# Two of the output sums of a seven-product channel mix move from VectorE to GpSimd

## The chip, the cores and the metric

The kernel runs on one core of one Trainium2 chip. The metric is the device time of one execution in microseconds (us). The kernel before takes 271.89 us, the median of three runs (271.51 to 272.08). The profiled execution of it has a span of 269.8 us, counted from its first to its last instruction; all times in the profile lines below are counted from that start.

A core has several engines that run side by side and wait for each other by semaphores: TensorE (PE in the profile, PEld for its weight loads) multiplies matrices into PSUM banks; VectorE (DVE), ScalarE (ACT) and GpSimd (POOL) do elementwise work; SyncE (SP) mostly issues DMA transfers.

## The reference

Eight batches of 576 tokens, 8 heads of 64. A linear attention with cosine weights gives x, and an MLP mixer follows: a token mix, a residual, a channel mix and a second residual.

```python
q_p = phi(q, cos_w, sin_w)            # relu(q) * cos, relu(q) * sin
k_p = phi(k, cos_w, sin_w)
kv  = np.einsum('bhsf,bhsd->bhfd', k_p, v)
num = np.einsum('bhsf,bhfd->bhsd', q_p, kv)
den = np.einsum('bhsf,bhf->bhs', q_p, k_p.sum(axis=2))[..., None] + 1e-06
x   = num / den                        # then heads side by side: [8, 576, 512]

h  = np.maximum(x.transpose(0, 2, 1) @ w_tok1, 0.0) @ w_tok2
u  = x + h.transpose(0, 2, 1)
h2 = np.maximum(u @ w_ch1, 0.0) @ w_ch2
return u + h2
```

The change concerns the last two lines: h1 = relu(u @ w_ch1) (1536 wide), the product h1 @ w_ch2, and the sum u + h2.

## The kernel before

512 tokens of each batch are worked on as one channel call; the remaining 64 tokens of all eight batches form a last call, the tail (`u_tail`). The first calls (batches 0 and 1) are written out in a list of operations; batches p = 2 to 7 and the tail go through `channel7`, seven calls in all. While the call of batch p runs, `hooks7` puts work of later batches into its slots: attention, token mix and residual of batch p + 1 (so for p = 2 to 6), features of q and k and the casts of v for batch p + 2 (p = 2 to 5), loads of batch p + 3.

`channel7` computes h1 @ w_ch2 in seven half-size products instead of eight (Winograd's form of Strassen's scheme). h1 is cut into four quadrants: a11 and a12 are the two channel halves of the upper 256 tokens, a21 and a22 those of the lower 256. The output tile u is cut into u11, u12, u21, u22 in the same way by tokens and output columns. Each quadrant of u is 128 x 512 in fp32.

```python
        for mi in range(NCH):                       # 12 up-projections, TensorE
            c_ps = psM.tile([P, 512], F32, name="c_ps", tag="psM")   # 4 banks in turn
            ...                                     # c_ps += wc1 x uT
            relu(by_slot[mi], h1[:, mi, :], c_ps)   # ScalarE or VectorE
            ...                                     # s1 = a21 + a22, s2 = s1 - a11 (VectorE, L652)
            step()                                  # the hooks of this slot
        Dk = bank()
        ...
            A = bank()
            product(A, a11, quad(0, 0), True)
            nc.scalar.copy(va, A)                   # L686
        nc.vector.tensor_sub(a21, a11, a21)         # L687
        step()
        product(Dk, a22, t4, True)
        nc.scalar.copy(vb, Dk)                      # L690
        nc.vector.tensor_sub(u22, u22, vb)          # L691
        step()
        Bk = bank()
        product(Bk, s2, t2, True)
        nc.vector.tensor_add(va, Bk, va)            # L695
        nc.vector.tensor_sub(s2, a12, s2)           # L696
        step()
        C = bank()
        product(C, s1, t1, True)
        nc.scalar.copy(vc, C)                       # L700
        nc.vector.tensor_add(u12, u12, va)          # L701
        nc.vector.tensor_add(u22, u22, vc)          # L702
        step()
        product(Dk, a21, t3, False)
        nc.vector.tensor_add(vb, Dk, va)            # L705
        step()
        wide = ...                                  # vb, read once for each column half
        u2 = ...                                    # u21 and u22 together
        product(C, s2, quad(1, 1), False)           # the sixth product: needs L696
        if fine:                                    # the tail
            nc.vector.tensor_add(u2, u2, wide)      # L711
            store(2, u, 2)
            nc.vector.tensor_add(u12, C, u12)       # L713
            store(0, u, 2, slice(D2, Dm))
            ...
            for jj in range(2):
                product(A, a12, quad(1, 0), False, (jj,))
                nc.vector.tensor_add(u11[:, jj], A[jj], u11[:, jj])   # L718
            ...
        else:
            nc.vector.tensor_add(u12, C, u12)       # L721
            step()
            product(A, a12, quad(1, 0), False)
            nc.vector.tensor_add(u11, A, u11)       # L724
            store(0, u, 2)
            nc.vector.tensor_add(u2, u2, wide)      # L726
            store(2, u, 2)
```

All matmuls of these products are at L657 in the profile, those of the up-projection at L667. The profile calls `va` w2r (it lives in the memory of that weight), a quadrant of h1 `h`, and s1 and s2 both `s`.

Other parts that matter here: the residual of the next batch and its bf16 cast for the transposing DMA, put in slots 10 and 11 of the call, just ahead of the seven products:

```python
        def uo(self, g):                            # VectorE, L466
            nc.vector.tensor_add(self.sb("u")[:, js, :], self.ps.pop(("u", g)), self.x[:, js, :])
        def ubc(self, g, eng="P"):                  # GpSimd, ub<-u
            copy(eng, self.sb("ub")[:, js, :], self.u[:, js, :])
        def utx(self, g):                           # SyncE, L473: uT<-ub, for the next call
            nc.sync.dma_start_transpose(...)
        def turnx(self, j, n):                      # SyncE, L355: qpT<-qp
            nc.sync.dma_start_transpose(...)
        def feat(self, t, j, g, f, eng): ...        # q and k features, ScalarE L331, VectorE L333
        def cast(self, a, n, g, eng): ...           # v to bf16, vbf<-vt, mostly GpSimd
```

The qp tile has one buffer: features of the next batch can be written only once the transposes have read it.

Of the kernel before, what the change touches and what calls it, by code (L numbers as in the profile page):

```python
# [59 lines left out]
def kernel(  # L60
# [11 lines left out]
    nc = tc.nc  # L72
# [555 lines left out]
    def channel7(uT, u, store, by_slot, hooks, fine=False):  # L628
# [3 lines left out]
        def step():  # L632
            nonlocal slot
            for f in hooks.get(slot, ()):
                f()
            slot += 1
# [8 lines left out]
        vb = one.tile([P, 2, D2], F32, name="vb")  # L645
        vc = one.tile([P, 2, D2], F32, name="vc")
        u11, u12 = u[:, 0:2, :D2], u[:, 0:2, D2:]
        u21, u22 = u[:, 2:4, :D2], u[:, 2:4, D2:]
# [39 lines left out]
        step()  # L688
        product(Dk, a22, t4, True)
        nc.scalar.copy(vb, Dk)  # L690
        nc.vector.tensor_sub(u22, u22, vb)  # L691
        step()
        Bk = bank()
        product(Bk, s2, t2, True)
# [4 lines left out]
        product(C, s1, t1, True)  # L699
        nc.scalar.copy(vc, C)  # L700
        nc.vector.tensor_add(u12, u12, va)  # L701
        nc.vector.tensor_add(u22, u22, vc)  # L702
        step()
        product(Dk, a21, t3, False)
        nc.vector.tensor_add(vb, Dk, va)  # L705
# [124 lines left out]
    for p in range(2, B):  # L830
        s = bt[p]
        n = bt[p + 1] if p + 1 < B else None
        m = bt[p + 2] if p + 2 < B else None
        nxt = p + 3 if p + 3 < B else None
        if p < QUADS:
            channel(s.uT, s.u, store_batch(p), evac, hooks_for(n, m, nxt))
        else:
            channel7(s.uT, s.u, store_batch(p), evac7 if n else evac2, hooks7(n, m, nxt, p == QUADS))
    channel7(uT_tail, u_tail, store_tail, evac2, {}, fine=True)

    _ = tile, bass_utils
# [30 lines left out]
```

## Time and profile before

| what | value |
|---|---|
| time, median of 3 runs | 271.89 us |
| span of the profiled execution | 269.8 us |
| granted TensorE clock | 0.993 |
| VectorE busy | 207.4 us, 381 instructions |
| GpSimd busy | 52.8 us, 68 instructions |
| L691, u22 - vb, p = 2 to 7 | 6 instructions, 8.3 us |
| L702, u22 + vc, p = 2 to 7 | 6 instructions, 4.1 us |
| the same two in the tail | 0.69 and 0.69 us |

How to read it: a busy share is an average over the whole span. A group line names the source line, the engine, the operation, out<-in, the shape, the count, the busy total, the mean in nanoseconds and the idle time ahead of it with what ended it. A line of the waits names who waited, for whom, for how long in total, how often, and the longest. A timeline line begins with start and duration in us. DVE instructions overlap by about 0.08 us where one follows another, so starts and ends touch with a small overlap.

### The profile page before, as it was taken

How to read it: one execution, taken by the hardware profiler on the slowest of the kernel's cores; microseconds unless marked ns; L12 is line 12 of the kernel's file. 1: busy time of each engine (PE TensorE's matmuls, PEld its weight loads, DVE VectorE, ACT ScalarE, POOL GpSimd, SP SyncE). 2: the span in 40 equal slices, each digit the busy share in tenths (PEclk: the TensorE clock that was granted, in tenths of full speed). 3: DMA queues.
4: the chain of work that ended last, by engine and by line, in shares of the span. 5: the costliest groups of instructions: out<-in, count | busy, mean ns of one | idle time of the engine just before them, and what ended most of it. 6: DMA issues, size and time to landing. Idle time of an engine off the chain costs nothing.

```text
span 269.8 us, 5452 instructions
## 1 busy us (share of the span) xinstructions
PE 255.2 (95%) x2165; PEld 160.9 (60%) x2181; DVE 207.4 (77%) x381; ACT 143.8 (53%) x236; POOL 52.8 (20%) x68
## 2 busy tenths in 40 slices
PE   6987999999999999999999999999999999999991
PEld 2875556456444556765676557655765575585580
DVE  6389798799791879969896869796968596584592
ACT  2886272384491577739772878287833423323410
POOL 2164060040023261202432013220300030000000
PEclk9999999999999999999999999999999999999997
DMA  6999999999999999799999995950492053003004
GB/s 201 358 234 155 254 255 209 345 252 232 332 294 181 304 374 360 137 166 331 268 334 183 317 362 119 169 186 2 92 222 116 0 80 156 19 2 156 0 2 157
DMA packets 79145, 53.41 MB, mean 198 GB/s; under 512 B 47760, under 2 KB 76688, under 8 KB 79120
## 3 DMA queue, kind: packets, MB, share of 16 engines
q1 hardware_dynamic: 74544, 48.77, 68.2%
q0 software_dynamic: 4144, 3.77, 9.3%
q10 hardware_dynamic: 432, 0.52, 0.5%
q8 instruction: 17, 0.28, 0.4%
q14 instruction: 8, 0.07, 0.1%
HBM read 35.85 MB, written 9.44 MB: 168 GB/s over the span
## 4 chain that ended last, share of the span: by engine, by line
PE 62%; DVE 22%; DMA 8%; issue 4%; ACT 1%; SPq 1%; DVEq 0%; ACTq 0%
PE c_ps L667 21%; PE m_ps L657 10%; PE c L513 8%; PE o L525 7%; DMA kt<-in_k_dram 6%; PE b L434 5%; DVE u L466 4%; DVE s L652 4%; PE kv L362 3%; DVE u L691 3%; PE nf L391 2%; DVE s L696 2%; PE u L461 2%; DVE kp L333 2%; DVE w2r L695 1%
## 5 line engine op out<-in xcount | busy, mean ns | idle before, releaser
L667 PE MATMUL c_ps<-uT,wc 128*128 128x512 bf16 x288 | 70.4, 379 | 0.6 <-ACT h L269 0.3
L269 ACT ACTIVATE h<-c_ps 128x512 bf16<-128x512 f32 x66 | 39.3, 595 | 52.5 <-PE c_ps L667 32.9
L667 PEld LDWEIGHTS <-wc 128*128 128x128 bf16 x336 | 30.9, 98 | 32.8 <-issue 0.6
L657 PEld LDWEIGHTS <-h 128*128 128x128 bf16 x336 | 32.9, 98 | 5.3
L265 POOL CAST ub<-u 128x1024 bf16<-128x1024 f32 x14 | 18.5, 1327 | 84.2 <-DVE u L466 45.6
L331 ACT ACTIVATE qp<-qt,cos_t 128x512 bf16<-128x512 f32 x33 | 23.3, 719 | 21.3 <-DMA qt<-in_q_dram 12.7
L657 PEld LDWEIGHTS <-s 128*128 128x128 bf16 x252 | 24.2, 98 | 6.8 <-DVE s L696 4.0
L271 DVE TENSOR_SCALAR h<-c_ps 128x512 bf16<-128x512 f32 x18 | 12.4, 689 | 20.1 <-PE c_ps L667 20.0
L265 POOL CAST vbf<-vt 128x512 bf16<-128x512 f32 (+3 forms) x28 | 18.1, 680 | 42.8 <-DMA vt<-in_v_dram 42.0
L657 PE MATMUL m_ps<-wc,s 128*128 128x256 bf16 x168 | 20.7, 273 | 2.6 <-DVE s L696 2.6
L513 PE MATMUL c<-uT,wc 128*128 128x512 bf16 x96 | 22.7, 379 | 0.1
L525 PE MATMUL o<-wc,h 128*128 128x512 bf16 x92 | 21.6, 379 | 0.2
L414 DVE TENSOR_TENSOR x<-nf,den 128x512 bf16<-128x512 f32 x30 | 20.7, 691 | 1.0
L331 ACT ACTIVATE qp<-qt,sin_t 128x512 bf16<-128x512 f32 x30 | 21.4, 722 | 0.0
L391 PEld LDWEIGHTS <-qpT 128*128 128x128 bf16 x320 | 15.2, 98 | 10.1 <-DVE x L414 1.5
L657 PE MATMUL m_ps<-wc,h 128*128 128x256 bf16 x168 | 20.6, 273 | 0.0
L657 PE MATMUL m_ps<-t,h 128*128 128x256 bf16 x168 | 20.6, 273 | 0.0
L434 PE MATMUL b<-x,w 128*128 128x512 bf16 (+1 forms) x84 | 19.8, 353 | 0.3
L466 DVE TENSOR_TENSOR u<-u,x 128x1024 f32<-128x1024 f32 x16 | 19.3, 1216 | 0.8 <-PE u L461 0.8
L331 ACT ACTIVATE kp<-kt,sin_t 128x512 bf16<-128x512 f32 x21 | 14.8, 714 | 3.1 <-DMA kt<-in_k_dram 3.1
L461 PE MATMUL u<-B,w 128*128 128x512 bf16 x64 | 16.1, 379 | 0.0
L333 DVE TENSOR_SCALAR kp<-kt,cos_t 128x512 bf16<-128x512 f32 x18 | 10.7, 599 | 6.7 <-DMA kt<-in_k_dram 6.7
(117 smaller groups left out, 375.8 us busy)
## 6 DMA issues: line engine op xcount, KB each, us to landing
out_dram<-u SPq DMA_DIRECT2D x32, 256.0 KB, 3.7
qt<-in_q_dram SPq DMA_DIRECT2D x8, 640.0 KB, 7.4
kt<-in_k_dram SPq DMA_DIRECT2D x8, 640.0 KB, 8.0
qt<-in_q_dram SPq DMA_DIRECT2D x8, 512.0 KB, 6.3
kt<-in_k_dram SPq DMA_DIRECT2D x8, 512.0 KB, 6.9
vt<-in_v_dram SPq DMA_DIRECT2D x6, 640.0 KB, 8.8
vt<-in_v_dram SPq DMA_DIRECT2D x6, 512.0 KB, 7.4
wc<-in_moe_w_ch_dram POOLq DMA_DIRECT2D x4, 384.0 KB, 8.7
```

What stands on the lines that cost most here:

```text
L265: (nc.scalar.copy if eng == "A" else ENG[eng].tensor_copy)(dst, src)
L269: nc.scalar.activation(dst, src, AF.Relu)
L331: nc.scalar.activation(dst, src, AF.Relu, scale=tab)
L391: nc.tensor.matmul(nm[:, hh * (D + 1):(hh + 1) * (D + 1)], self.qpT[:, j * H + h, :], self.kv[:, h, :D + 1], start=(not eps or hh == 0), s ...
L414: nc.vector.tensor_mul(dst, nmv[:, :, :, :D], den_b)
L434: nc.tensor.matmul(b1[:, mi], w1[:, col(self.c, j), mi * P:(mi + 1) * P], self.x[:, j, cs], start=(j == 0 and (g == 2 or mi == 0)), stop=( ...
L461: nc.tensor.matmul(ps[:, jj], w2[:, ki, 1 + 2 * g + jj, :], self.B1[:, ki, :], start=(ki == 0), stop=(ki == NT - 1))
L466: nc.vector.tensor_add(self.sb("u")[:, js, :], self.ps.pop(("u", g)), self.x[:, js, :])
L513: nc.tensor.matmul(ps, wc1[:, ki, mi * P:(mi + 1) * P], self.uT[:, :, ki, :], start=(ki == 0), stop=(ki == NCC - 1))
L525: nc.tensor.matmul(self.ps["o", j], self.h1[:, ki, j * P:(j + 1) * P], wc2[:, ki, :], start=(ki == 0), stop=(ki == NCH - 1))
L657: nc.tensor.matmul(ps[jj] if isinstance(ps, list) else ps[:, jj], a[:, ki, jj * P:(jj + 1) * P], b[:, ki], start=(first and ki == 0 and (j ...
L667: nc.tensor.matmul(c_ps, wc1[:, ki, mi * P:(mi + 1) * P], uT[:, :, ki, :], start=(ki == 0), stop=(ki == NCC - 1))
```

## The change

Two of the output sums, u22 = u22 - vb and u22 = u22 + vc, are computed by GpSimd instead of VectorE, at the same places of the program. All their inputs and their output lie in SBUF, which GpSimd can read: ScalarE has already copied the PSUM banks into vb and vc. Everything else stays, the last sum of that quadrant included (`u2 += wide`, on VectorE, L726 or L711), which now waits for GpSimd. It is for taking work from VectorE, which in this phase also prepares the operands a21 and s2 of the later products, and giving it to an engine that has less to do.

```diff
         step()
         product(Dk, a22, t4, True)
         nc.scalar.copy(vb, Dk)
-        nc.vector.tensor_sub(u22, u22, vb)
+        nc.gpsimd.tensor_sub(u22, u22, vb)
         step()
         Bk = bank()
         product(Bk, s2, t2, True)
@@
         product(C, s1, t1, True)
         nc.scalar.copy(vc, C)
         nc.vector.tensor_add(u12, u12, va)
-        nc.vector.tensor_add(u22, u22, vc)
+        nc.gpsimd.tensor_add(u22, u22, vc)
         step()
         product(Dk, a21, t3, False)
         nc.vector.tensor_add(vb, Dk, va)
```

## Prediction

> **What bounds the kernel now.** I read the page's busy shares first, then the waits of TensorE, then the timeline around one such wait, then the places where a gain could be lost again.
>
> ```profile
> PE 255.2 (95%) x2165; PEld 160.9 (60%) x2181; DVE 207.4 (77%) x381; ACT 143.8 (53%) x236; POOL 52.8 (20%) x68
> ```
>
> TensorE is the bound: 255.2 of 269.8 us. A change on VectorE can only shorten the time where TensorE stands still for VectorE. The waits of TensorE name one such place:
>
> ```profile
> PE m_ps L657 <- DVE s L696: 2.6, 5, 0.5
> ```
>
> That is the sixth product, C += s2 x quad(1,1), which waits for s2 = a12 - s2 (L696). Five waits: channel calls p = 2 to 6. The timeline of VectorE, GpSimd and TensorE in p = 4 (columns: start, duration, engine and line; in brackets the idle time before):
>
> ```profile
> 163.53 0.94 DVE L687 TENSOR_TENSOR h<-h 128x1536 bf16<-128x1536 bf16 x1
> 163.67 1.70 POOL L265 CAST ub<-u 128x1024 bf16<-128x1024 f32 x1 [1.48 <-DVE u L466]
> 164.39 1.52 DVE L691 TENSOR_TENSOR u<-u,vb 128x512 f32<-128x512 f32 x1
> 165.44 1.47 PE L657 MATMUL m_ps<-t,h 128*128 128x256 bf16 x12
> 165.83 0.68 DVE L695 TENSOR_TENSOR w2r<-m_ps,w2r 128x512 f32<-128x512 f32 x1
> 166.43 0.94 DVE L696 TENSOR_TENSOR s<-h,s 128x1536 bf16<-128x1536 bf16 x1
> 167.43 1.48 PE L657 MATMUL m_ps<-wc,s 128*128 128x256 bf16 x12 [0.52 <-DVE s L696]
> ```
>
> L691, the first of the two moved sums, takes 1.52 us here; in p = 7 and the tail, where no cast runs beside it, the same shape takes 0.69. The cast ends at 165.37 and L691 at 165.91, 0.54 us later: L691 stood blocked behind the cast, as the cast had been blocked behind L687 (alone it takes 1.11). L691 then pushes L695 and L696, and TensorE starts the product at 167.43. Products follow each other every 1.31 us elsewhere (161.51, 162.82, 164.13, 165.44), so its free start would be 166.75: 0.68 us lost per call, of which the profile calls 0.52 idle because the last matmul's end is modelled.
>
> **What the Trainium skill says.** "SBUF — State Buffer", section "Who interferes with whom": VectorE and GpSimd share one port pair, and a VectorE instruction with two SBUF inputs and a GpSimd instruction that reads SBUF exclude each other for the whole instruction; one with a single SBUF input is free of it. The trace agrees: L691 above, and L695 and L705, one input from PSUM, stay at 0.68. "GPSIMD Engine Reference", section "3.1 Elementwise — side-by-side cycle accounting": an fp32 add of 2048 elements per partition takes 4497 ns on GpSimd. The only two-input operation on GpSimd before is bf16:
>
> ```profile
> L625 POOL TENSOR_TENSOR t<-wc 128x1536 bf16<-128x1536 bf16 x1 | 3.1, 3099 | 9.2 <-DVE wc L624 9.2
> ```
>
> 3099/1536 gives 2.02 ns per element, the skill's figure 2.2; for 512 elements an estimate of 1.03 to 1.12 us, I take 1.1. "Perfetto Trace Analysis", section "Optimizing Scalar/DVE Operations", warns that offloading between these two engines might not help, because of that port. Who gets the port when both wait is decisive here. The trace shows it in p = 3, VectorE against five casts in a row:
>
> ```profile
> 126.12 3.66 POOL L265 CAST vbf<-vt 128x512 bf16<-128x512 f32 x5 [6.87 <-DMA vt<-in_v_dram]
> 126.43 0.83 DVE L333 TENSOR_SCALAR kp<-kt,sin_t 128x512 bf16<-128x512 f32 x1
> 127.19 0.82 DVE L333 TENSOR_SCALAR kp<-kt,cos_t 128x512 bf16<-128x512 f32 x1
> 127.93 0.83 DVE L333 TENSOR_SCALAR kp<-kt,sin_t 128x512 bf16<-128x512 f32 x1
> ```
>
> Alone these take 0.48 and a cast 0.57; together one of each passes every 0.75 us. They alternate: neither keeps the port for its next instruction.
>
> **The change, part by part.** Seven calls, two sums each: 14 instructions leave VectorE (L691 8.3 + 0.7 us, L702 4.1 + 0.7 us, 13.8 of its 207.4 us) and add 14 x 1.1 = 15.4 us to GpSimd's 52.8. Neither total sets the end; the six steps below do.
>
> (1) p = 4 without L691: L695 needs only its product, started 162.82; in p = 7 it starts 1.51 us after that start (237.66 to 239.17), so about 164.4, right after L687, and ends at 165.1. L696 then wants the port, held by the cast until 165.37. By alternation it is next. L691 needed 0.54 us after release for 512 f32 elements; L696 streams for about 0.80 (its 0.94 less the same 0.15), so it ends at 166.2. TensorE can start at 166.75 with 0.5 us to spare: gain 0.68 us at each of the five waits, at most 3.4 us.
>
> (2) GpSimd's subtraction then runs 166.2 to 167.3 and blocks L701 (two SBUF inputs), which ends near 167.8. L705 and L721 follow, to 168.4 and 169.05; the banks they free are wanted from 169.8 on. GpSimd's addition runs 167.8 to 168.9; L726 cannot start before L724, near 170.2. Cost on the path: none.
>
> (3) p = 2 and p = 3: what comes next waits for DMA. TensorE's next channel call starts at 142.69 and needs uT, whose second transpose, issued at 137.59, took 4.8 us to land: 142.4. It stands behind loads issued from 125.87 to 132.22, the last landing at 140.5, and the SyncE queue runs from 111.84 to there with hardly a pause, before the first gain arises. Then:
>
> ```profile
> 140.50 7.04 SPq L355 DMA_TRANSPOSE qpT<-qp x3
> 149.62 0.72 ACT L331 ACTIVATE qp<-qt,cos_t 128x512 bf16<-128x512 f32 x1 [3.14 <-DMA qpT<-qp]
> 150.88 1.02 PE L667 MATMUL c_ps<-uT,wc 128*128 128x512 bf16 x4 [0.29 <-ACT h L269]
> ```
>
> The last qpT transpose lands at 149.4, ScalarE's feature waits for it, the relu after it frees the bank that TensorE waits for. These times belong to the DMA queue. The 1.36 us of p = 2 and 3 turn into longer waits between 142 and 151; I count 0.
>
> (4) p = 4: uT lands at 168.6 against a new start of 169.8, no wait. But the third qpT transpose again lands by its own clock, 172.48 + 3.7 = 176.2; ScalarE's feature starts at 176.36, the relu behind it ends at 177.57, and the seventh up-projection, at 177.97 now, cannot start before about 177.6. So 0.35 of 0.68 us stays.
>
> (5) p = 5 and 6: no q features follow, uT of the last lands at 222.7 against a new start of about 224: 0.68 each, 1.36 us.
>
> (6) p = 7 and tail: TensorE does not wait there for L696, so nothing is gained. The tail ends on VectorE:
>
> ```profile
> 260.06 0.58 ACT L700 COPY vc<-m_ps 128x512 f32<-128x512 f32 x1 [2.09 <-PE m_ps L657]
> 260.17 0.68 DVE L701 TENSOR_TENSOR u_tail<-u_tail,w2r 128x512 f32<-128x512 f32 x1
> 260.77 0.69 DVE L702 TENSOR_TENSOR u_tail<-u_tail,vc 128x512 f32<-128x512 f32 x1
> 261.37 0.68 DVE L705 TENSOR_TENSOR vb<-m_ps,w2r 128x512 f32<-128x512 f32 x1
> 262.09 1.22 DVE L711 TENSOR_TENSOR u_tail<-u_tail,vb 128x1024 f32<-128x1024 f32 x1
> ```
>
> L702 fills a pause: L705's product lets it start at 261.3 anyway. On GpSimd the addition waits for vc (260.64) and the port (260.8) and ends near 261.9; L711 needs it. A tie at 1.1 us; every tenth above delays the end. I book +0.1.
>
> Sum: -(0 + 0.35 + 1.36) + 0.1 = -1.6; 271.89 - 1.6 = 270.3 us.
>
> **Rivals.** *GpSimd keeps the port*: its subtraction is ready when the cast ends, and if it goes first, L696 ends at about 165.4 + 1.1 + 0.8 = 167.3, as before; the time stays at 271.9, or, if the addition also slipped ahead, L696 would be 1 us later than now and the five calls would cost up to 5 us, 276 us. The alternation in p = 3 speaks against it, though those were other operations. *All five gains survive*: 271.89 - 3.4 = 268.5; this needs the loads of p = 3 to move up with TensorE, and the queue ahead of them is not waiting for TensorE. *The tail pays*: if the f32 addition takes 1.5 us, L711 starts 0.4 later and the result is 270.6. *VectorE as a bound that is relieved everywhere*: 77% busy, the wrong reading, since 13.8 us of relief meets only five short waits.
>
> **Range and chances.** Centre 270.3. Below it the share of the DMA-bound gain that may survive, down to 268.9; above it the port going the other way, up to 271.9. Two per cent is 5.4 us, more than all waits on L696 together, so faster by that much is nearly excluded, and slower needs the worst port order five times.
>
> **What would show it.** In the changed profile the wait of TensorE for L696 should be gone; L696 should end within 0.9 us of the ub cast's end; L701 should be stretched to over 1.4 us by the GpSimd subtraction; waits for uT or qpT should grow between 142 and 151 us; the uT call after p = 6 should start 1.5 to 1.8 us earlier. GpSimd's 128x512 f32 sums should show near 1.1 us. I am wrong if L696 stays behind the subtraction, if those sums are far from 1.1 us, or if the DMA stretch moves up with the rest.

## The result and the profile after

The changed kernel takes 270.06 us (median of 4 runs, 269.80 to 270.46) against 271.70 us for the kernel before, measured beside it (271.24 to 272.08). The ratio is 0.9942 with a 95% interval of 0.9921 to 0.9963: faster by 1.6 us, or 0.6%. In a second set of runs, beside other kernels, the ratio was 0.9938 (0.9917 to 0.9960); by the medians the gain was 1.2 us there (270.38 against 271.62).

The busy shares of the changed kernel:

```profile
PE 254.9 (95%) x2165; PEld 161.5 (60%) x2181; DVE 202.3 (76%) x367; ACT 143.8 (54%) x236; POOL 76.7 (29%) x82
```

VectorE has 14 instructions fewer but only 5.1 us less busy time, not 13.8; GpSimd has 23.9 us more, not 15.4. Most of the difference is time in which an instruction stands blocked and counts as busy: on VectorE five L701 (1.75 us instead of 0.68) and five L696 (1.17 instead of 0.94) make 6.5 of the 8.7 us. On GpSimd the sums are also longer than estimated when nothing blocks them (1.27 us, not 1.1). TensorE's work is unchanged. Its waits from p = 2 on are other ones:

```profile
PE c_ps L667 <- DMA uT<-ub: 1.0, 2, 0.6
PE c_ps L667 <- ACT h L269: 0.9, 2, 0.5
...
PE nf L391 <- DMA qpT<-qp: 0.2, 1, 0.2
```

The five waits for s2 (L696) are gone. In their place stand 2.1 us of waits that lead back to the transposing DMAs; the kernel before had 0.3 us of these. The timeline around the seven products of p = 4, VectorE, GpSimd, TensorE (start, duration, engine and line):

```profile
162.88 1.70 POOL L265 CAST ub<-u 128x1024 bf16<-128x1024 f32 x1 [1.47 <-DVE u L466]
...
163.61 0.69 DVE L695 TENSOR_TENSOR w2r<-m_ps,w2r 128x512 f32<-128x512 f32 x1
...
164.22 1.17 DVE L696 TENSOR_TENSOR s<-h,s 128x1536 bf16<-128x1536 bf16 x1
164.55 1.97 POOL L691 TENSOR_TENSOR u<-u,vb 128x512 f32<-128x512 f32 x1
...
164.65 1.47 PE L657 MATMUL m_ps<-t,h 128*128 128x256 bf16 x12
...
165.31 1.75 DVE L701 TENSOR_TENSOR u<-u,w2r 128x512 f32<-128x512 f32 x1
...
165.96 1.47 PE L657 MATMUL m_ps<-wc,s 128*128 128x256 bf16 x12
166.60 1.60 POOL L702 TENSOR_TENSOR u<-u,vc 128x512 f32<-128x512 f32 x1
```

Read it as a relay: VectorE and GpSimd take turns at the port that the prediction describes. The cast ends at 164.58; L696, waiting since 164.22, ends 0.81 us later, at 165.39. Only then does the subtraction get through, though it had been issued at 164.55: it ends at 166.52, 1.13 us after L696. L701 waits for it, ends at 167.07, and the addition follows to 168.20. TensorE's sixth product starts at 165.96, 1.31 us after the fifth (164.65), with no pause. The timeline also shows what does not wait: L695, with one input from PSUM and one from SBUF, takes 0.69 us in the middle of the cast.

Where did the five gains go? TensorE's start times in the two traces, after minus before, in us:

| call | first product | sixth product | first up-projection of the next call | its seventh |
|---|---|---|---|---|
| p = 2 | -0.47 | -1.15 | -0.65 | -0.65 |
| p = 3 | -0.64 | -1.33 | -0.94 | -0.78 |
| p = 4 | -0.79 | -1.47 | -1.49 | -0.78 |
| p = 5 | -0.79 | -1.46 | -1.47 | -1.47 |
| p = 6 | -1.47 | -2.15 | -2.17 | -2.17 |

The span ends 2.10 us earlier (267.7 against 269.8). The first 0.47 us is there before any moved sum runs, so this pair of executions differs by that for other reasons. Without it 1.63 us are left, as in the medians; but a stretch that waits for DMA can swallow a head start too, so this subtraction is not exact. Each row gains 0.67 to 0.69 us from the first product to the sixth. The lines that give it back, TensorE in the calls p = 3, 4 and 5 of the changed kernel:

```profile
114.95 1.04 PE L667 MATMUL c_ps<-uT,wc 128*128 128x512 bf16 x4 [0.56 <-DMA uT<-ub]
...
141.75 1.02 PE L667 MATMUL c_ps<-uT,wc 128*128 128x512 bf16 x4 [0.45 <-DMA uT<-ub]
...
145.99 0.43 PE L391 MATMUL nf<-kv,qpT 128*128 128x65 bf16 x8 [0.22 <-DMA qpT<-qp]
...
150.10 1.02 PE L667 MATMUL c_ps<-uT,wc 128*128 128x512 bf16 x4 [0.32 <-ACT h L269]
...
177.19 1.02 PE L667 MATMUL c_ps<-uT,wc 128*128 128x512 bf16 x4 [0.54 <-ACT h L269]
```

A second profile of the changed kernel, from the second set of runs, has the same head start (0.48 us at the first product of p = 2) and gives the gains back at other places:

```profile
122.73 1.02 PE L667 MATMUL c_ps<-uT,wc 128*128 128x512 bf16 x4 [0.57 <-ACT h L269]
...
142.72 1.02 PE L667 MATMUL c_ps<-uT,wc 128*128 128x512 bf16 x4 [1.12 <-DMA uT<-ub]
...
151.01 1.02 PE L667 MATMUL c_ps<-uT,wc 128*128 128x512 bf16 x4 [0.45 <-ACT h L269]
...
177.78 1.02 PE L667 MATMUL c_ps<-uT,wc 128*128 128x512 bf16 x4 [0.21 <-ACT h L269]
```

There the start at 142.72 is 0.03 us later than before, and p = 4 begins its products at 160.33, 0.13 us later: the gains of p = 2 and 3 and the head start are all gone. At 177.78 TensorE is 0.19 us ahead, so 0.32 us of p = 4 is kept; p = 5 and 6 keep 0.69 us each, and the span ends 1.50 us earlier (268.3).

In the first profile, the wait at 177.19 is for a relu that stands on ScalarE behind a q feature, and that feature waits for the third qpT transpose:

```profile
175.93 0.72 ACT L331 ACTIVATE qp<-qt,cos_t 128x512 bf16<-128x512 f32 x1 [3.12 <-DMA qpT<-qp]
```

The tail of the changed kernel:

```profile
257.89 0.58 ACT L700 COPY vc<-m_ps 128x512 f32<-128x512 f32 x1 [2.09 <-PE m_ps L657]
...
258.62 1.27 POOL L702 TENSOR_TENSOR u_tail<-u_tail,vc 128x512 f32<-128x512 f32 x1 [1.47 <-ACT vc L700]
...
259.22 0.69 DVE L705 TENSOR_TENSOR vb<-m_ps,w2r 128x512 f32<-128x512 f32 x1 [0.46 <-PE m_ps L657]
260.01 1.23 DVE L711 TENSOR_TENSOR u_tail<-u_tail,vb 128x1024 f32<-128x1024 f32 x1
```

The addition ends at 259.89 and L711 starts at 260.01; by the 0.08 us overlap of one VectorE instruction with the next, L705 (to 259.91) alone would let it start at about 259.83. Measured against TensorE's last product the end comes 0.07 us later than before.

### The profile page after: what moved, and what is told of

Read it like the earlier page. It is cut to its first block, busy times and chain, and to the rows that moved or that the text cites. A ratio compares the mean times of both kernels' runs of the same rounds, so it can differ in the third digit from the quotient of the medians.

```text
span 267.7 us, 5480 instructions
## 1 busy us (share of the span) xinstructions
PE 254.9 (95%) x2165; PEld 161.5 (60%) x2181; DVE 202.3 (76%) x367; ACT 143.8 (54%) x236; POOL 76.7 (29%) x82
## 4 chain that ended last, share of the span: by engine, by line
PE 67%; DMA 12%; issue 5%; POOL 4%; DVE 4%; SPq 4%; ACT 1%; DVEq 0%; POOLq 0%; ACTq 0%
PE c_ps L667 20%; PE m_ps L657 16%; PE c L513 5%; PE b L434 5%; PE o L525 4%; DMA uT<-ub 4%; PE kv L362 3%; PE u L461 3%; POOL ub L265 3%; DMA qpT<-qp 3%; DMA vt<-in_v_dram 3%; DMA kt<-in_k_dram 3%; PE wm L193 3%; PE tr L312 2%; SPq L144 2%
## 5 line engine op out<-in xcount | busy, mean ns | idle before, releaser
L265 POOL CAST vbf<-vt 128x512 bf16<-128x512 f32 (+3 forms) x28 | 18.7, 703 | 39.9 <-DMA vt<-in_v_dram 38.3
L331 ACT ACTIVATE kp<-kt,cos_t 128x512 bf16<-128x512 f32 x22 | 15.4, 719 | 0.3 <-DMA kt<-in_k_dram 0.3
```

The source lines that it names most:

```text
L265: (nc.scalar.copy if eng == "A" else ENG[eng].tensor_copy)(dst, src)
L331: nc.scalar.activation(dst, src, AF.Relu, scale=tab)
```

## The experiments

The theory: what pays is that the blocked subtraction no longer stands ahead of s2 on VectorE; the engine that does it is of no account, and most of the gain of p = 2 to 4 is lost to DMA. The rivals: the relief of VectorE as a whole pays; the sums must leave VectorE; the gain is small for a reason other than DMA. All ratios are to the kernel before, measured beside each set.

**Only the subtraction on GpSimd.**

```diff
-        nc.vector.tensor_sub(u22, u22, vb)
+        nc.gpsimd.tensor_sub(u22, u22, vb)
```

> Only the subtraction u22 - vb goes to GpSimd; the addition stays on VectorE. Theory (what counts is that the blocked subtraction no longer stands ahead of the s2 operand on VectorE): all of the gain of the change, 270.0 us, ratio to the kernel before about 0.994; no wait of TensorE for the s2 subtraction, its five waits of 0.52 us gone. Rival (relief of VectorE as a whole counts, 13.8 us for both sums): the subtraction is two thirds of it, so about two thirds of the gain, 270.6 us.

Measured: 269.32 us, ratio 0.9924 (0.9897 to 0.9951). The waits for L696 are gone. The interval contains the whole gain of the change (0.9942), and two thirds of it (0.996) lie outside. Moving the addition as well bought nothing that can be seen.

**Only the addition on GpSimd.**

```diff
-        nc.vector.tensor_add(u22, u22, vc)
+        nc.gpsimd.tensor_add(u22, u22, vc)
```

> Only the addition u22 + vc goes to GpSimd. Theory (it stands behind the s2 operand on VectorE, so it is on no path): no gain, 271.7 us, ratio 1.000, the five waits of 0.52 us for the s2 operand stay; the tail may lose 0.1 us. Rival (relief of VectorE counts): a third of the gain, 271.1 us, ratio 0.998.

Measured: 275.95 us, ratio 1.0192 (1.0152 to 1.0232): 4.35 us slower. Both the theory and the rival missed it. Its waits, and the timeline of p = 4:

```profile
PE m_ps L657 <- DVE s L696: 7.9, 5, 1.6
```

```profile
165.18 1.52 DVE L691 TENSOR_TENSOR u<-u,vb 128x512 f32<-128x512 f32 x1
...
167.15 1.26 POOL L702 TENSOR_TENSOR u<-u,vc 128x512 f32<-128x512 f32 x1 [0.99 <-ACT vc L700]
167.22 2.01 DVE L696 TENSOR_TENSOR s<-h,s 128x1536 bf16<-128x1536 bf16 x1
...
169.28 1.48 PE L657 MATMUL m_ps<-wc,s 128*128 128x256 bf16 x12 [1.58 <-DVE s L696]
```

With the subtraction left in its old place, s2 is late, and vc becomes ready just before it. The addition takes the free port at 167.15, s2 asks 0.07 us later and stands blocked until 168.41; it takes 2.01 us instead of 0.94. TensorE's wait grows from 0.52 to 1.58 us, five times 1.06 us or 5.3 us. Of these 0.7 us is absorbed in the call of p = 4: from its first to its seventh up-projection the kernel before takes 8.19 us, with its waits on transposes, and this one 7.48. So an instruction that stands behind s2 in the program is not behind it at the port once it is on another engine. In the change it cannot get ahead: s2 is done at 165.39, vc is ready only at 165.49, and on GpSimd the subtraction comes first.

**Nothing on GpSimd; the subtraction behind s2 on VectorE.**

```diff
         product(Dk, a22, t4, True)
         nc.scalar.copy(vb, Dk)
-        nc.vector.tensor_sub(u22, u22, vb)
@@
         nc.vector.tensor_sub(s2, a12, s2)
+        nc.vector.tensor_sub(u22, u22, vb)
```

> Nothing goes to GpSimd; on VectorE the subtraction u22 - vb is only put behind the s2 operand. Theory (place in VectorE's queue, not the engine, makes the gain): the same gain as the change, 270.0 us, ratio 0.994, the s2 operand again 1.2 us long because it waits for the cast's port, the moved subtraction 0.69 us. Rival (the work has to leave VectorE): at most a small gain, 271 us or more, since VectorE has the same busy time as before.

Measured: 269.33 us, ratio 0.9926 (0.9901 to 0.9951). VectorE in p = 4 (the lines are one up from L695 on, s2 is L695, the subtraction L696):

```profile
164.02 1.17 DVE L695 TENSOR_TENSOR s<-h,s 128x1536 bf16<-128x1536 bf16 x1
165.11 0.68 DVE L696 TENSOR_TENSOR u<-u,vb 128x512 f32<-128x512 f32 x1
```

The same gain with the same engine: TensorE's waits for s2 are gone, s2 is 1.17 us as in the change, and the sums stay at 0.68 us where GpSimd needs 1.27 unblocked. The place in VectorE's queue makes the gain.

**The second cast on ScalarE, all sums where they were.** The transposing DMA goes with the cast, and the first qpT transpose stays behind it.

```diff
-            at(11, n.u_all, 1)
+            at(11, n.um, 1)
+            at(11, n.uo, 1)
+            at(13, n.ubc, 1, "A")
+            at(13, n.utx, 1)
@@
-            at(12, m.turnx, 0, 2)
+            at(13, m.turnx, 0, 2)
```

> All sums stay on VectorE in the old order; instead the second bf16 cast of the residual goes from GpSimd to ScalarE, behind its copy of the second product, and its transposing DMA with it. Theory (the port held by the cast is what stretched the subtraction from 0.69 to 1.52 us): the subtraction is back at 0.69 us, the s2 operand ends about 0.8 us earlier, the five waits of 0.52 us vanish, gain as in the change or up to 0.5 us more because the transposes are issued some 0.7 us earlier: 269.5 to 270.1 us. Rival (the length of VectorE's queue itself, not the port): the waits stay above 0.2 us and the time above 271 us. ScalarE could give some back, it gets about 1.0 us more per call.

Measured: 268.74 us, ratio 0.9900 (0.9876 to 0.9924). The timeline of p = 4:

```profile
163.34 1.05 ACT L265 CAST ub<-u 128x1024 bf16<-128x1024 f32 x1 [0.17 <-DVE u L466]
...
163.97 0.68 DVE L691 TENSOR_TENSOR u<-u,vb 128x512 f32<-128x512 f32 x1
...
165.17 0.94 DVE L696 TENSOR_TENSOR s<-h,s 128x1536 bf16<-128x1536 bf16 x1
...
166.31 1.47 PE L657 MATMUL m_ps<-wc,s 128*128 128x256 bf16 x12
```

With the cast off the port, the subtraction is back at 0.68 us, s2 at 0.94, and the product starts 1.31 us after the one before it (165.00), although VectorE does every instruction it did before in the same order. So it was the cast on GpSimd that held the subtraction up. The gain, 2.9 us, is larger than the 1.5 to 2.1 us expected; the second uT transpose is also issued sooner after the first (2.6 us instead of 3.2), and whether that is the reason was not tried. Here too one large wait came up, TensorE for uT near 142 us:

```profile
PE c_ps L667 <- DMA uT<-ub: 1.3, 1, 1.3
```

**The DMA left out, without and with the change.** Two kernels leave out, in the calls p = 2 to 7, the loads of q, k and v of later batches and the transposes qpT<-qp; batches 4 to 7 are then computed from stale data, with all arithmetic in place.

```diff
-        if nxt is not None:
-            at(0, load, nxt, "k")
-            at(0, load, nxt, "q")
-            at(16 if nxt == 5 else 9, load, nxt, "v")
@@
-            at(12, m.turnx, 0, 2)
-            at(14, m.turnx, 2, 2)
-            at(15, m.turnx, 4, 1)
+            m.qpT = bt[3].qpT
```

> The kernel before, but in the calls p = 2 to 7 the loads of q, k and v of later batches and the transposes qpT<-qp are left out, so batches 4 to 7 are computed from stale data; all arithmetic stays. It is the partner of the next run. Theory: the waits of TensorE for the s2 operand stay at five times 0.5 us, waits on DMA between 140 and 151 us vanish; 270 to 271.5 us.

> The changed kernel with the same loads and transposes left out. Theory (in the full kernel the gain of p = 2, 3 and 4 is given back to waits for uT and qpT): here all five gains of 0.68 us survive, so it is 3.2 to 3.5 us faster than its partner, ratio of the two about 0.988. Rival (the gain is small for another reason than DMA): the difference to the partner stays at 1.6 to 2.1 us.

Measured: 270.74 us (ratio 0.9968, 0.9954 to 0.9982) without the change and 266.95 us (0.9820, 0.9788 to 0.9851) with it. The change is now worth 3.8 us by the medians and 2.8 us by the two profiled spans (268.26 and 265.45), nearly or more than twice the 1.6 us of the full kernel. Single runs of the second kernel lie between 266.3 and 268.2, so the exact value is open; both values are outside the 1.6 to 2.1 us of the rival. The waits of TensorE, first without the change, then with it:

```profile
PE m_ps L657 <- DVE s L696: 3.0, 5, 0.9
```

```profile
PE c_ps L667 <- DMA uT<-ub: 0.7, 1, 0.7
```

In p = 3 to 6 the gain survives now in full, 0.69 us in each of p = 4, 5 and 6 between the two traces and 1.06 us in p = 3, where the wait for s2 was 0.89 us long. The gain of p = 2 is still given back: in p = 2 the second uT transpose took 4.7 us to land instead of 3.0, though the last load had landed 10 us before. That was seen in p = 2 of the changed kernel too (4.9 us against 3.2), but not in its second profile (3.2 us). What slows it is open.

**The v load of batch 6 behind the transposes**, on top of the cast on ScalarE.

```diff
-            at(16 if nxt == 5 else 9, load, nxt, "v")
+            at(16 if nxt in (5, 6) else 9, load, nxt, "v")
```

> All sums on VectorE in the old order, the second cast of the residual on ScalarE as in the run with the cast on ScalarE, and the v load of batch 6 moved from slot 9 to slot 16 of p = 3, so that it stands behind the transposes uT and qpT in the queue and no longer ahead of them. Theory (the transposes of p = 3 are late because they queue behind that load): the wait of 1.26 us for uT near 142 us shrinks below 0.3 us, and the time falls to 267.0 to 267.9 us. Rival (the transposes are late because of the k and q loads, or are slow by themselves): the wait stays above 0.8 us and the time at 268.7.

Measured: 267.81 us, ratio 0.9853 (0.9822 to 0.9884). The SyncE queue around 130 us, first with the cast on ScalarE alone, then with the load late as well:

```profile
128.76 3.04 SPq L144 DMA_DIRECT2D vt<-in_v_dram  x2
133.15 6.79 SPq L473 DMA_TRANSPOSE uT<-ub  x2
140.03 7.09 SPq L355 DMA_TRANSPOSE qpT<-qp  x3
```

```profile
133.84 3.84 SPq L473 DMA_TRANSPOSE uT<-ub  x2
137.78 6.94 SPq L355 DMA_TRANSPOSE qpT<-qp  x3
144.77 1.30 SPq L144 DMA_DIRECT2D vt<-in_v_dram  x2
```

The uT transposes land after 4.0 and 3.3 us instead of 7.8 and 5.3, and the wait near 142 us is gone. Two others stand in the next call, 0.62 us for uT at 168.38 and 0.49 us for a relu at 176.50: there the load of batch 7 is now ahead of the uT transposes, which take 6.4 and 5.4 us to land.

**Both v loads behind the transposes**, on top of that.

```diff
-            at(16 if nxt in (5, 6) else 9, load, nxt, "v")
+            at(16, load, nxt, "v")
```

> As the run with the v load of batch 6 in slot 16, and the v load of batch 7 in slot 16 of p = 4 as well. In that run two waits were left after the attention list: 0.62 us for uT near 168 us and 0.49 us for a relu near 176 us. Theory (the first is again the queue of loads ahead of the transposes): the wait near 168 is gone, 0.4 to 0.7 us off, 267.2 us. Rival: the transposes of p = 4 are slow without loads ahead of them, the wait stays and the time is 267.8.

Measured: 266.77 us, ratio 0.9822 (0.9791 to 0.9854), the fastest kernel of the study: 4.4 us below the kernel before (271.15 in this set). From p = 2 on TensorE has no wait left that the profile names:

```profile
PE wm L193 <- DVE par_i L163: 2.3, 1, 2.3
PE tr L346 <- DVE qp L333: 0.8, 1, 0.8
PE nm L391 <- DVE x L414: 0.7, 1, 0.7
PE uT L451 <- DVE B L271: 0.6, 1, 0.6
PE nm L391 <- ACT kv L265: 0.3, 1, 0.3
```

All five end before 26 us. The waits for uT and for the relu went together when one load was moved, so both came from that load standing ahead of transposes in the queue.

**The q features later as well**, on top of that.

```diff
-            for i, slot in enumerate((1, 2, 3, 4, 5, 6, 9, 10, 11, 12)):
+            for i, slot in enumerate((3, 4, 5, 6, 7, 7, 9, 10, 11, 12)):
```

> As the run with both v loads late, and the first six q features of each call two or more slots later, so that the relus of the first up-projections do not stand behind a q feature that waits for the qpT transpose. Theory (ScalarE's order, not the transpose itself, makes TensorE wait near 176 us): that wait of 0.5 us is gone and the time is 0.3 to 0.6 us below the run with both v loads late. Rival: the features get in the way of later relus and the transposes of the next batch are issued later; same or slower by up to 1 us.

Measured: 266.94 us, ratio 0.9836 (0.9805 to 0.9867), no difference from the run before it. The wait that this was to remove had already vanished, so the run says nothing about ScalarE's order as its cause.

**The change once more**, beside the last kernels.

> The changed kernel once more, beside the others on one chip. Theory: the same as the runs with only the subtraction on GpSimd or only put later on VectorE, within 0.5 us; ratio to the kernel before 0.991 to 0.996.

Measured: 270.38 us, ratio 0.9938 (0.9917 to 0.9960). It agrees with its first measurement. Its median is 1.06 us above those of the two single moves (269.32 and 269.33, from another set), more than the 0.5 us expected, but the intervals of the ratios overlap; that the single moves are better is not shown.

## Why the prediction was right

The predicted 270.3 us (-1.6) met 270.06 us (-1.64). That the two agree so closely is partly luck, since the second set gives -1.2 us. The mechanism holds step by step:

- **Step 1, alternation at the port and 0.68 us at each wait: right.** L696 ends 0.81 us after the cast, as worked out, ahead of the subtraction that was queued too, in all five calls. The fifth to sixth product spacing is 1.31 us in each. The run with the cast on ScalarE shows the cast on GpSimd to be the cause.
- **Step 2, nothing new on the path: right.** L701 is stretched to 1.75 us and the addition ends at 168.2, before L726 may start. The size was off: 1.27 us for an unblocked sum on GpSimd, not 1.1. With 3.09 us for 1536 bf16 elements, 1.27 us for 512 fp32 ones is a quarter more than a third of the long operation; whether type or a fixed part makes it was not tried.
- **Step 3, the 1.36 us of p = 2 and 3 lost to DMA: right in kind.** The term was 0. The first profile gives about -0.3 us (from -0.47 to -0.78 in the table), because the DMA stretch moved up a little (the second uT transpose of p = 3 lands at 141.61 instead of 142.43); the second gives nothing, even the head start is gone. The runs without loads and transposes and the late v loads show the cause in p = 3. The gain of p = 2 was mostly lost earlier than predicted, at 114.95 or 122.73 and not between 142 and 151; in the first profile by a slow uT transpose that the prediction did not have, and whose cause is not the loads.
- **Step 4, 0.35 us left of p = 4: right in the second profile, about 0 in the first.** In the second the third qpT transpose lands at 176.34 (predicted 176.2) and 0.32 us is kept. In the first the call began 0.79 us earlier, and that transpose, issued at 170.86, took 4.9 us instead of 3.7 and landed only 0.43 us earlier, at 175.75: 0.36 us late by the call's own clock, just what was to stay.
- **Step 5, 1.36 us in p = 5 and 6: right**, 0.67 and 0.68. The up-projections after p = 6 start 2.17 us earlier in the first profile and 1.58 us in the second; 1.5 to 1.8 was predicted.
- **Step 6, the tail, +0.1: right**, 0.07 us measured.

Two points of step 1 need a limit. The order also fits a simpler rule than alternation, that whoever asks first goes first: s2 asks at 164.22, and GpSimd can issue the subtraction only at 164.55; with the addition alone on GpSimd a lead of 0.07 us decides. No run tells the two rules apart. And the lines of the prediction do not show that an instruction with one input from PSUM is spared, since at its L695 (165.83) the cast had ended (165.37). The changed kernel shows it: L695 takes 0.69 us beside the cast and L705 0.68 us beside the addition. One input from SBUF alone is no safe sign, though: L333, which has a single tensor input, in SBUF, was stretched from 0.48 to 0.83 us by the casts in p = 3.

How the loss splits between steps 3 and 4 thus differs from one execution to the next; in the first profile an excess in step 3 and a shortfall in step 4 cancel. The first rival was dismissed correctly for the change, but it describes what the addition alone does: there GpSimd takes the port first, s2 comes about 1 us later, and the time goes to 276 us, the number that the prediction gave for an addition that slips ahead.

## What to carry to other kernels

Ask of an instruction on a busy engine not how long it is but what stands behind it: here moving one line further down in VectorE's program gave all that the second engine gave. Between VectorE and GpSimd the order at the shared port is part of the schedule, and an instruction moved to GpSimd can overtake the critical one it used to follow. When TensorE is at 95%, look first at what the next wait will be; two loads moved behind the transposes, with one cast moved off the port, were worth more than twice the change.

## What was not expected of the hardware

A lead of 0.07 us at the port cost VectorE 1.07 us (2.01 instead of 0.94), nearly the whole length of the GpSimd sum. Most uT transposes took 3.0 to 3.5 us to land, a few 4.0 to 5.1 us although the loads had landed, for reasons that no run shows, and up to 7.8 us when plain loads stood ahead of them in SyncE's queue. Where the two engines met at the port, busy time grew on both sides: 14 sums of 1.27 us each when unblocked, 17.8 us, show as 23.0 us on GpSimd in the changed kernel, and six L701 as 9.4 us instead of 4.1.
